# A fused adaLN block on one Trainium2 core: shift and scale moved to the features, projections with half-row pairs, gate rows in four column tiles, and a new list of steps

## The chip, the cores and the metric

The kernel runs on one core of a Trainium2 chip. A core has a matrix engine (TensorE, PE in the profile, with its weight loads shown apart as PEld), a vector engine (VectorE, DVE), a scalar engine (ScalarE, ACT), GpSimd (POOL) and SyncE (SP), which here issues nearly all DMA transfers. The metric is the device time of one execution in microseconds; 416.89 is the median before.

## What is computed

Everything is bfloat16, for one batch of 2048 tokens with 576 features and 32 heads of 18:

```python
mod = (silu(c) @ w_mod)            # six rows of 576: sa, ca, ga, sb, cb, gb
h = layernorm(x) * (1 + ca) + sa
q, k, v = split(h @ wqkv)          # 32 heads of 18
phi(t) = concat(softmax(t @ w_phi), softmax(-(t @ w_phi)))
o = phi(q) @ (phi(k).T @ v) / (phi(q) @ sum(phi(k)))
x = x + ga * (o @ wo)
h = layernorm(x) * (1 + cb) + sb
x = x + gb * (relu(h @ w1) @ w2)   # 576 -> 4608 -> 576
```

The attention is linear: the keys of all tokens are summed into one small matrix per head before any query can be finished. So all 16 tiles of 128 tokens go through the norm, the key and value projections and the key softmax first. Then the queries and the FFN run in blocks of two tiles.

## The kernel before

**Two parts.** The first is a list of short steps, written out by hand as a string (L900) and run through a table of lambdas (L857): DMA loads, folding of weights, norms, projections, key softmax, key-value sums, and attention and FFN of the first block. The second, `block(n)` (L928), runs the other seven blocks in loops. The scheduler is off for SyncE, TensorE, VectorE and ScalarE (`manual_schedule`), so each of these engines executes its instructions in the order of the list. An instruction that waits holds up all that is behind it on its engine, and nothing on another unless it waits for that one. The order between engines comes from semaphores alone.

**Folded weights.** The query and key weights are multiplied by `w_phi` on the chip: the raw key weights are transposed on TensorE (`fold_T`, L333; the query weights arrive transposed by DMA, `load_turned`, L156), multiplied with a block-diagonal `wbd` (`fold`, L343), and copied out (`fold_out`, L350). The factor 1 + ca is then multiplied into the rows of the folded weights and of the value weights (`fold_scale`, L355, steps SC1, SCv, SC0), and the shift sa is turned into one row per weight (`fold_bias`, L362, steps B1, Bv, B0; copied by BE1, BEv, BE0) that sits in row 64 of the fifth chunk. The normalised tile has a one in column 576 to meet it. The 576 features are thus four chunks of 128 rows and a fifth of 64 rows, padded with the shift row and zeros.

**The norm.** Statistics per tile on VectorE (LS, L217), the root on ScalarE (RS, L223), the normalisation per pair of tiles on VectorE (LX, L227). Tiles 0 to 3 are transposed on TensorE (PT, L248) and copied out by ScalarE and VectorE (PTA, PTB); tiles 4 to 15 by DMA (LT, L242). The features hT1 have three buffers of four tiles.

**Projections.** `project` (L546) makes K, V or Q of one tile: two halves of the columns by five chunks, ten matmuls into one of three PSUM buffers (`mmp`, L74; L425 in the profile). ScalarE copies each out (KE, VE, QE). K and Q have column parts of 270 and 306, V of 288 and 288.

**Key softmax.** Per block of four tiles: minimum and maximum trees (MN, MX), differences (LO, HI) on VectorE, exponentials on ScalarE (EX, L484), sums on TensorE (SU, L491), the last addition (SA), reciprocals on ScalarE (RC), scaling on VectorE (SC). Steps with q do the same for the queries of a block. KVa to KVc sum keys times values (L603), KVE copies them out. NU, NUE, OT, OTE, WO, WOE carry the first block on; S2, R2, X2, PN, PNE are its second norm; G and FW are its FFN (L785, L793).

**Gates.** The gate ga is multiplied into the columns of `wo` (`wo_scale`, L390), gb into the FFN's output. Both rows are needed on all partitions, so a matmul with the SiLU vector repeated 128 times (`crep`) makes each (`mod_row`, L377, steps RA and RB; L382 in the profile).

In the FFN, the chunk of 64 rows is already handled in pairs (`f1_pairs`, L780; `wo_pair`, L686): two matmuls of 64 rows each, one on the upper and one on the lower half of the array's rows, into different PSUM banks.

## Time and profile before

| | us |
|---|---|
| median of three runs | 416.89 (416.82 to 417.81) |
| the profiled execution | 416.77 |
| its span, first to last instruction | 414.8 |
| TensorE busy | 406.0 |
| VectorE busy | 237.0 |
| ScalarE busy | 173.8 |
| first K projection starts | 16.26 |
| key-value sums start | 84.68 |
| first FFN matmul starts | 103.61 |

Rows of groups give line, engine, operation, the tiles written and read, shapes and count, then the time in which the group was busy, the mean duration of one in ns, and the idle time of the engine just before them with what ended it. In a timeline the first two columns are start and length. The length of a merged row reaches to the end of its last instruction, and matmuls overlap, so the cost of a matmul in a stream is read from one start to the next. A row of a stretch gives its bounds and length, then busy time and count of TensorE, of its weight loads, of VectorE, ScalarE and GpSimd, then the granted TensorE clock (1.00 is full), the DMA share and GB/s.

### The profile page before, as it was taken

The numbers are of one execution on the slowest core, as the hardware profiler recorded it, in microseconds if no ns is written. First come the engines' busy times: TensorE is split into PE (matmuls) and PEld (weight loads), VectorE is DVE, ScalarE is ACT, GpSimd is POOL, SyncE is SP. The second block draws the span as 40 slices with busy tenths as digits, with TensorE's granted clock in tenths as the row PEclk, the third lists the DMA queues.
The fourth block names the chain that finished last, engine by engine and source line by source line (L and its number), as shares of the span: only waits on it lengthen the run. The fifth ranks groups of instructions, "written<-read, shape, count | busy, mean of one in ns | idle before, by whom it ended". The sixth has DMA issues, their size and how long they took to land.

```text
span 414.8 us, 9278 instructions
## 1 busy us (share of the span) xinstructions
PE 406.0 (98%) x3993; PEld 332.4 (80%) x3993; DVE 237.0 (57%) x617; ACT 173.8 (42%) x280; POOL 12.0 (3%) x39
## 2 busy tenths in 40 slices
PE   6899999999999999999999999999999999999997
PEld 4777877787887888788878887888888788878876
DVE  7989999988855554637345552746192533230011
ACT  4787889954861064006302630452055014302400
POOL 8100000000000000000000000000000000000000
PEclk9999999999999999999999999999999999999999
DMA  8959665079561420613051014203210501210000
GB/s 254 255 142 276 127 176 120 2 188 363 204 163 27 101 63 2 83 48 33 12 107 32 16 33 85 46 2 67 65 34 2 115 17 32 14 33 16 2 0 30
DMA packets 70513, 35.12 MB, mean 85 GB/s; under 512 B 55305, under 2 KB 68106, under 8 KB 70474
## 3 DMA queue, kind: packets, MB, share of 16 engines
q1 hardware_dynamic: 69872, 34.52, 35.3%
q8 instruction: 31, 0.51, 0.5%
q10 hardware_dynamic: 602, 0.02, 0.1%
q14 instruction: 8, 0.07, 0.0%
...
## 4 chain that ended last, share of the span: by engine, by line
PE 94%; DVE 3%; DMA 1%; ACT 1%; issue 0%; SPq 0%; ACTq 0%
PE ps_y L836 34%; PE ps_h L793 31%; PE ps_q L425 5%; PE ps_v L425 4%; PE ps_h L785 4%; PE ps_k L425 4%; PE ps_sum L491 3%; PE ps_wo L701 3%; PE ps_wo L425 2%; PE ps_kv L603 1%; PE ps_num L644 1%; DMA wk_raw<-in_A_wqkv_dram 1%; PE ps_wT L337 1%; PE ps_row L382 1%; DVE xn L229 1%
## 5 line engine op out<-in xcount | busy, mean ns | idle before, releaser
L798 ACT ACTIVATE H<-ps_h 128x1024 bf16<-128x1024 f32 x72 | 73.6, 1022 | 170.8 <-PE ps_h L785 120.9
L836 PE MATMUL ps_y<-w_sb,H 128*128 128x288 bf16 (+2 forms) x1188 | 143.0, 282 | 0.0
L836 PEld LDWEIGHTS <-H 128*128 128x128 bf16 x1188 | 113.7, 98 | 27.3
L793 PE MATMUL ps_h<-hT,w1a 128*128 128x256 bf16 x640 | 74.9, 273 | 0.4 <-DVE hT L396 0.4
L793 PEld LDWEIGHTS <-w1a 128*128 128x128 bf16 x640 | 61.2, 98 | 10.1 <-issue 2.8
L844 DVE TENSOR_TENSOR outt<-ps_y,row_gb 128x288 bf16<-128x288 f32 (+2 forms) x33 | 14.8, 448 | 86.8 <-PE ps_y L836 86.8
L793 PE MATMUL ps_h<-hT,w1b 128*128 128x256 bf16 x512 | 59.0, 273 | 0.0
L425 PEld LDWEIGHTS <-hT 128*128 128x128 bf16 x480 | 46.1, 97 | 12.7 <-issue 0.9
L793 PEld LDWEIGHTS <-w1b 128*128 128x128 bf16 x512 | 49.8, 98 | 6.6 <-issue 0.6
L706 DVE TENSOR_TENSOR x_sb<-x_sb,ps_wo 128x288 bf16<-128x288 bf16 x28 | 12.7, 454 | 33.5 <-PE ps_wo L701 24.8
L220 DVE BATCH_NORM_STATS2 bst<-x_sb 128x6 f32<-128x288 bf16 x64 | 25.6, 442 | 0.2
L229 DVE TENSOR_SCALAR xn<-x_sb,mv,rstd 128x576 bf16<-128x576 bf16 x32 | 12.2, 424 | 21.7 <-ACT rstd L225 21.6
L425 PE MATMUL ps_v<-wv_sb,hT 128*128 128x288 bf16 x160 | 21.6, 286 | 0.3 <-ACT wv_sb L358 0.3
L425 PE MATMUL ps_k<-wfold,hT 128*128 128x270 bf16 (+1 forms) x160 | 21.4, 285 | 0.4 <-ACT wfold L86 0.4
L425 PE MATMUL ps_q<-wfold,hT 128*128 128x270 bf16 (+1 forms) x160 | 21.4, 285 | 0.0
L502 DVE TENSOR_REDUCE ln_s<-room 128x66 f32<-128x1188 bf16 x14 | 19.1, 1368 | 3.3 <-ACT room L484 3.3
L785 PE MATMUL ps_h<-hT,w1c 64*128 64x256 bf16 x288 | 19.9, 271 | 0.0
L484 ACT ACTIVATE room<-room 128x1188 bf16<-128x1188 bf16 x16 | 18.9, 1196 | 0.5
L484 ACT ACTIVATE phik<-phik 128x2376 bf16<-128x2376 bf16 x8 | 17.5, 2184 | 0.4 <-DVE phik L457 0.4
L785 PEld LDWEIGHTS <-w1c 64*128 64x128 bf16 x288 | 12.1, 94 | 5.1 <-issue 3.8
L444 DVE TENSOR_TENSOR tree<-tree 128x264 bf16<-128x264 bf16 (+2 forms) x48 | 14.6, 304 | 1.7
L396 DVE TENSOR_SCALAR hT<-hT,mod 128x256 bf16<-128x256 bf16 x35 | 9.7, 343 | 6.4 <-DMA hT<-xn 6.4
...
## 6 DMA issues: line engine op xcount, KB each, us to landing
...
```

Of the source, the lines that this page charges most:

```text
L220: V.bn_stats(out=st[:, half, :], in_=x_sb[:, t0 + j, half * 288:(half + 1) * 288])
L229: V.tensor_scalar(out=xn[:, j, 0:D], in0=x_sb[:, t0 + j, :], scalar1=mv[:, j, 0:1], scalar2=rs[:, j:j + 1], op0=ALU.subtract, op1=ALU.mult)
L425: T_.matmul(ps[:, 0:cn], lhsT=lhs[:, ci, :], rhs=w[:, ci, cs:cs + cn], start=(ci == 0), stop=(ci == KC - 1))
L444: V.tensor_tensor(out=a[:, :, 0:w], in0=a[:, :, 0:w], in1=a[:, :, w:2 * w], op=op)
L484: A_.activation(out=E[:, j:j + k], in_=E[:, j:j + k], func=ACT.Exp)
L502: V.tensor_reduce(out=t["l", b][:, k * 22:(k + 1) * 22].rearrange("p (g s) h -> p g s h", s=2), op=ALU.add, axis=mybir.AxisListType.X, in_ ...
L706: V.tensor_tensor(out=xs[:, cs:cs + cn], in0=xs[:, cs:cs + cn], in1=p[:, 0:cn], op=ALU.add)
L785: T_.matmul(f1[q][:, e, hh * w:hh * w + w], lhsT=w1["c"][r, 2 * q + hh, :], rhs=hT[r, 4, :], start=(first and hh == 0), stop=(not first an ...
L793: T_.matmul(f1[q][:, e, hh * w:hh * w + w], lhsT=w1_at(2 * q + hh, e, ci), rhs=hT[:, ci, :], start=(first and hh == 0 and ci == 0), stop=( ...
L798: A_.activation(out=p2t["H1"].rearrange("p (e j) n -> p e j n", e=2)[:, :, 2 * q:2 * q + 2], in_=f1[q][:].rearrange("p e (h n) -> p e h n" ...
L836: T_.matmul(ps[:, 0, 0:cn], lhsT=p2t["H1"][:, k, j * P:(j + 1) * P], rhs=p2t["w2"][:, k, c], start=(k == 0), stop=(k == NJ - 1))
L844: V.tensor_tensor(out=o[:, c], in0=ps[:, 0, 0:cn], in1=rows["gb"][:, c], op=ALU.mult)
```

## The change

The features are cut differently: chunks begin at 0, 128, 256, 320 and 448, and the third holds 64 features (256 to 319) twice, on the lower and the upper 64 partitions. The normalised tile is written with these 64 columns doubled (`spread`), per tile and on VectorE or ScalarE, so its transpose has them on both halves. Folding writes the middle chunk twice in two column tiles, and the loads follow the new cut.

Shift and scale are applied to the transposed features: for tiles 0 to 3 while they leave PSUM (PX, per pair of tiles and chunk), for the others in place (MH, per block and chunk). The steps SC1, SCv, SC0, B and BE are gone, and `wfold` and `wv_sb` are filled directly. A fourth buffer for the features of the last block is taken from the ET buffers.

`project` takes two (tile, kind) numbers: 0 to 15 are K, 16 to 31 V, 32 to 47 Q, step J.a.b. It runs the eight whole matmuls of the first, the pair of half-row matmuls of the first, the pair of the second, and its eight whole ones. The pair uses the two row halves for the two column halves.

The two gate rows become one step (RW): four column tiles of 32, each a half of ga or gb, then one copy (RWE), a store of four rows to DRAM and two broadcast loads (RD.2, RD.0, RD.1). The gate scaling of `wo` is two operations instead of five. The list is a new one throughout; the loops after it are as they were.

```diff
+CS = [0, 128, 256, 320, 448]
+CK = [P, P, 64, P, P]
+HC = 2
...
+    def load_values(i):
+        if i < 2:
+            rows = A_wqkv[i * 320:i * 320 + 256, 2 * D:].rearrange("(k p) n -> p k n", p=P)
+            nc.sync.dma_start(wv_sb[:, 3 * i:3 * i + 2, :], rows)
+        else:
+            for h in range(2):
+                cols = slice(2 * D + h * 288, 2 * D + h * 288 + 288)
+                nc.sync.dma_start(wv_sb[h * 64:h * 64 + 64, HC, h * 288:h * 288 + 288], A_wqkv[256:320, cols])
 
...
+        def spread(j, eng):
+
+            row = x_sb[:, t0 + j, :]
+            src = bass.AP(row.tensor, row.offset, [list(row.ap[0]), [256, 2], [1, 320]])
+            dst = xn[:, j, :].rearrange("p (a n) -> p a n", a=2)
+            if eng is A_:
+                nm = work.tile([P, 1], FP32, name="nm", tag="nm", bufs=4)
+                V.scalar_tensor_tensor(out=nm[:], in0=mv[:, j, 0:1], scalar=-1.0, in1=rs[:, j:j + 1], op0=ALU.mult, op1=ALU.mult)
+                A_.activation(out=dst, in_=src, func=ACT.Identity, scale=rs[:, j:j + 1], bias=nm[:])
+            else:
+                V.tensor_scalar(out=dst, in0=src, scalar1=mv[:, j, 0:1], scalar2=rs[:, j:j + 1], op0=ALU.subtract, op1=ALU.mult)
+
...
     def hT_of(b):
+        if b == 3 and b not in hT1:
+            t = work.tile([P, NG, U, P], BF16, name="hT3", tag="ET", bufs=2)
+            hT1[b] = t[:].rearrange("p g u c -> p (g u c)")[:, 0:KC * TPB * P].rearrange("p (k n) -> p k n", k=KC)
         if b not in hT1:
...
+    def ln1_out(u, ci, eng):
         c0 = u % 2 * U * P
-        for c1, c2 in parts:
-            copy(eng, hT_of(u // 2)[:, c1:c2, c0:c0 + U * P],
-                 psT[u][:, c1 * U * P:c2 * U * P].rearrange("p (k n) -> p k n", n=U * P))
-
+        modulate(eng, hT_of(u // 2)[:, ci, c0:c0 + U * P], psT[u][:, ci * U * P:(ci + 1) * U * P], mod[1], ci)
+
+    def ln1_mod(b, ci, eng):
+        modulate(eng, hT1[b][:, ci, :], hT1[b][:, ci, :], mod[1], ci)
 
...
-            for ck in range(KC):
-                o = (ck * 2 + r) * D + ci * P
-                T_.matmul(mod_ps[1][:, r * KC + ci:r * KC + ci + 1], lhsT=wma_[:, o:o + P], rhs=siluc[:, ck, :],
-                          start=(ck == 0), stop=(ck == KC - 1))
+            for p in range(0, P, CK[ci]):
+                for ck in range(KC):
+                    o = (ck * 2 + r) * D + CS[ci]
+                    T_.matmul(mod_ps[1][p:p + CK[ci], r * KC + ci:r * KC + ci + 1], lhsT=wma_[:, o:o + CK[ci]], rhs=siluc[:, ck, :],
+                              start=(ck == 0), stop=(ck == KC - 1))
+
+    mod[1] = const.tile([P, 2, KC], FP32, name="mod1")
...
         for g in range(NGR):
             nf = G6 if g < 5 else 2 * DH
-            T_.matmul(ps[0:KK[ci], g // 4, (g % 4) * G6:(g % 4) * G6 + nf], lhsT=wT[which][0:G6, g, ci * P:ci * P + KK[ci]],
-                      rhs=wbd[0:G6, g, 0:nf], start=True, stop=True)
+            for p in range(0, P, CK[ci]):
+                T_.matmul(ps[p:p + CK[ci], g // 4, (g % 4) * G6:(g % 4) * G6 + nf], lhsT=wT[which][0:G6, g, CS[ci]:CS[ci] + CK[ci]],
+                          rhs=wbd[0:G6, g, 0:nf], start=True, stop=True)
 
...
+    def gate_rows():
+        ps = rows["ps"] = mm_tile("ps_row")
+        for ck in range(KC):
+            for k in range(4):
+                o = k // 2 * 3 * D + k % 2 * 288
+                T_.matmul(ps[k * 32:k * 32 + 32, 0, 0:288], lhsT=crep[:, ck, :], rhs=wmb[:, ck, o:o + 288],
                           start=(ck == 0), stop=(ck == KC - 1))
 
-    def mod_row_out(name):
-        r = const.tile([P, D], BF16, name=f"row_{name}")
-        copy(A_, r[:].rearrange("p (a n) -> p a n", a=2), rows[name][:, :, 0:288])
-        rows[name] = r
-
-    def wo_scale(ci):
-        V.tensor_tensor(out=wo_sb[:, ci, :], in0=wo_sb[:, ci, :], in1=rows["ga"][:], op=ALU.mult)
+    def gate_rows_out(eng):
+        rows["four"] = wqp.tile([P, 288], BF16, name="row_four")
+        copy(eng, rows["four"][:], rows["ps"][:, 0, 0:288])
+
+    def gate_row(i):
+        if i == 2:
+            nc.sync.dma_start(four_d[:], rows["four"][0:P:32, :])
+            return
+        name = ("ga", "gb")[i]
+        r = rows[name] = const.tile([P, D], BF16, name=f"row_{name}")
+        nc.sync.dma_start(r[:].rearrange("p (a n) -> p a n", a=2), four_d[2 * i:2 * i + 2].unsqueeze(0).to_broadcast([P, 2, 288]))
+
+    def wo_scale(i):
+        c = slice(0, 2) if i == 0 else slice(2, KC)
+        V.tensor_tensor(out=wo_sb[:, c, :], in0=wo_sb[:, c, :], op=ALU.mult,
+                        in1=rows["ga"][:].unsqueeze(1).to_broadcast([P, c.stop - c.start, D]))
 
...
-    def project(name, t, w):
-        b, j = t // TPB, t % TPB
-        ps = pss[name, t] = mm_tile("ps_" + name)
-        proj((ps[:, 0], ps[:, 1]), hT1[b][:, :, j * P:(j + 1) * P], w, HALVES if name == "v" else PARTS)
+    WSRC = (("k", wfold[1], PARTS), ("v", wv_sb, HALVES), ("q", wfold[0], PARTS))
+
+    def project(*at):
+
+        def opened(k):
+            kind, w, splits = WSRC[k // NT]
+            t = k % NT
+            ps = pss[kind, t] = mm_tile("ps_" + kind)
+            return ps, hT1[t // TPB][:, :, t % TPB * P:t % TPB * P + P], w, splits
+
+        def whole(ps, lhs, w, splits, first):
+            for i, (cs, cn) in enumerate(splits):
+                for ci in (0, 1, 3, 4):
+                    T_.matmul(ps[:, i, 0:cn], lhsT=lhs[:, ci, :], rhs=w[:, ci, cs:cs + cn],
+                              start=(first and ci == 0), stop=(not first and ci == 4))
+
+        def pair(ps, lhs, w, splits, first):
+            for i, (cs, cn) in enumerate(splits):
+                r = slice(i * 64, i * 64 + 64)
+                T_.matmul(ps[:, i, 0:cn], lhsT=lhs[r, HC, :], rhs=w[r, HC, cs:cs + cn], start=first, stop=not first)
+
+        open_ = []
+        for k in at[:-1]:
+            open_.append(opened(k))
+            whole(*open_[-1], True)
+        last = opened(at[-1])
+        for p in open_:
+            pair(*p, False)
+        pair(*last, True)
+        whole(*last, False)
...
+    LP.1 LP.0 LK.1 LS.0 LS.2 WT.4 LK.0 WT.1 LH WBD WTE.4.1 WTE.1.1 WT.3 WTE.3.1 LS.1 RS.0 LP4.2 LS.3 F1.4 SIL
+    LS.4 RS.1 FB1.4.1 Z.11 Z.10 WT.0 F1.3 FA1.4.1 LX.1 LS.6 LS.7 LK.2 LA.0 LA.1 LV.0 Z.4 F1.1 FA1.3.1 FB1.3.1
+    MC1.0 LX.3 WTE.0.1 LX.0 WT.2 FA1.1.1 FB1.1.1 MSH WTE.2.1 F1.0 FA1.0 RS.3 MC1.1 FB1.0.1 MSC PT.0 PX.0.0.1
+    PX.0.3.1 Z.0 LQ.5 LX.2 PT.1 PX.0.4 LQ.0 LQ.1 F1.2 PX.1.1.1 OPEN CR PX.1.0 PX.0.2 LP4.4 PX.0.1.1 LV.1 PM.2
+    PM.1 PX.1.2 PM.0 PX.1.4 FB1.2 PX.1.3.1 FA1.2.1 J.0.1 KE.0 LX.7.1 LV.2 KE.1 J.16.17 LS.5 LX.6.1 VE.0 RS.2
+    LQ.3 LQ.2 LS.8 LS.9 LQ.4 F0.2 LS.10 LS.11 F0.0 RS.4 VE.1 FA0.2.1 LX.5 FB0.2 F0.3 LX.8.1 FA0.0 FB0.0 FB0.3.1
+    FA0.3.1 LX.9.1 RS.5 LP4.6 LX.4 LS.15 LS.14 LT.7 LT.6 LS.13 J.2.3 LT.5 LT.4 KE.2 LM.1 KE.3 J.18.19 VE.2
+    MH.1.0 MH.1.1 MH.1.3.1 VE.3 F0.1 FB0.1.1 FA0.1.1 MH.1.4 MH.1.2 J.6.7 KE.6 MN.0 KE.7 LX.10 LT.8 LT.9 LT.10
+    LX.11.1 F0.4 FB0.4.1 FA0.4.1 LS.12 J.4.5 KE.4 RS.7 J.34.35 MX.0 LO.0 MC2.3 LX.15 KE.5 RS.6 QE.2 LT.11 MH.2.0
+    MH.2.1 MH.2.4.1 QE.3 LX.14.1 J.32.33 MH.2.2.1 LX.12.1 MC2.0 MC2.2 LM.2 LO.1 MC2.4 MH.2.3 LX.13 LT.13 QE.1
+    MN.1 QE.0 HI.0 J.10.11 KE.10 J.8.9 EX.0 KE.8 KE.11 LO.2 KE.9 MX.1 LO.3 HI.3 SU.0 EX.3 LT.15 J.26.27 LT.14
+    LT.12 MH.3.1 qMX.0 PM.3 HI.1 SA.0 MH.3.0 MC2.1 LM.0 RW VE.10 MH.3.4 MH.3.2 MH.3.3.1 VE.11 J.12.13 MCE2 HI.2
+    SU.3 RC.0 MN.2 W1 RWE.1 LO.5 MX.2 KE.12 EX.2 KE.13 J.14.15 SA.3 SC.0 KE.14 RD.2 KE.15 qHI.0 J.20.21 VE.4
+    RC.3 LO.4 HI.5 HI.4 qMN.0 qLO.0 VE.5 EX.1 SU.2 J.22.23 VE.6 EX.5 J.30.31 VE.14 VE.7 SA.2 SU.5 qEX.0 VE.15
+    EX.4 qEX.1 MN.3 MX.3 J.24.25 LO.7 VE.8 HI.7 SC.3 RC.2 SU.1 LW.1.1 J.28.29 SA.1 VE.12 SA.5 RC.5 LO.6 HI.6
+    RC.1 VE.9 SU.4 LW.0.0 SC.5 qSU.0 qSA.0 SA.4 LW.2.0 EX.6 SC.2 EX.7 RD.0 VE.13 WOL qMN.1 RC.4 RD.1 qRC.0
+    J.40.41 QE.8 QE.9 SU.6 SU.7 SC.1 J.44.45 SA.6 qSC.0 SA.7 SC.4 KVa QE.12 RC.6 QE.13 SC.6 RC.7 SC.7 KVb KVc
+    KVE.0.1 WS.0 J.42.43 QE.10 KVE.1 qT.0 WS.1 NU.0 NUE.0 qLO.1 NU.1 QE.11 LW.1.0 J.38.39 QE.6 OT.0 NUE.1 OT.1
+    qMX.1 OTE.0 WO.0 OTE.1 WO.1 WOE.0 QE.7 J.36.37 QE.4 WOE.1 S2.1 S2.0 R2 QE.5 J.46.47 QE.14 X2 LW.2.1 P2
+    W2.1.1 LW.0.1 LW.3.0 PN PNE qMX.2 qHI.1 QE.15 G.0 W2.2.0 FW.2 RL.0 qEX.2 RL.2 W2.1.0 qEX.3 qMN.2 FW.1 RL.1
+    qHI.2 G.1 qSD.2 W2.0.0 qSD.3 qRC.1 RL.3 FW.4 LW.3.1 W2.0.1 FW.5 qSC.1 qT.1 qLO.2 RL.4 qEX.5 RL.5 G.2 RL.6
+    FW.8 NV.0 NVE.0 FW.7 Y.0.0.0 OU.0 NV.1 RL.7 NVE.1 OU.1 W2.2.1 Y.0.0.1 WP.0 Y.1.0.0 Y.1.0.1 WPE.0 qEX.4 RL.8
+    WP.1 Y.0.0.2 qSD.4 S3.0 Y.1.1.0 qSD.5 Y.1.1.1 WPE.1 S3.1 R3 qRC.2 YE.0.0 Y.1.0.2 Y.0.1.0 qSC.2 X3 XT MD.2
+    MD.3 Y.1.1.2 Y.0.1.1 qT.2 YE.1.0 MD.1 MD.4 Y.0.1.2 MD.0 YE.1.1 YE.0.1
```

In the new list a trailing .1 of a copying or modulating step means ScalarE and its absence VectorE.

More of the change, by code (lines that the diff above doesn't have):

```diff
@@ L371, in fold_bias_out @@
-    def fold_bias_out(which, dst, half, eng):
-        p = 64 - half * 64
-        copy(eng, dst[64:65, 4, half * 288:(half + 1) * 288], pool_tiles["B", which][p:p + 1, half, 0:288])
-    rows = {}
-    def mod_row(name, i):
-        ps = rows[name] = mm_tile("ps_row")
-        for half in range(2):
-            for ck in range(KC):
-                o = i * D + half * 288
-                T_.matmul(ps[:, half, 0:288], lhsT=crep[:, ck, :], rhs=wmb[:, ck, o:o + 288],
-                          start=(ck == 0), stop=(ck == KC - 1))
```

104 lines of the change are left out of this document (26 added, 78 removed).

## The prediction, as put on record

> **What bounds the kernel now.** I read the busy shares first, then the stretches between landmarks, then the groups, then the TensorE timeline around the few places where it already works in parts of its array.
>
> ```profile
> PE 406.0 (98%) x3993; PEld 332.4 (80%) x3993; DVE 237.0 (57%) x617; ACT 173.8 (42%) x280; POOL 12.0 (3%) x39
> PE 94%; DVE 3%; DMA 1%; ACT 1%; issue 0%; SPq 0%; ACTq 0%
> ```
>
> TensorE is busy for 98% and carries 94% of the chain that ended last, at a granted clock of 1.0 throughout. So TensorE time taken out counts, as long as nothing else is late. The stretches (first column the time, then TensorE, its weight loads, VectorE, ScalarE) show where that is tight:
>
> ```profile
> 16.26:28.56 12.30, 11.82 (x111) 9.44 (x111) 11.12 (x33) 10.24 (x29) 0.62 (x3) 1.00 0.72 175
> 28.56:54.03 25.47, 25.47 (x254) 20.06 (x252) 24.15 (x65) 18.78 (x43) 1.03 (x3) 1.00 0.74 177
> 54.03:84.68 30.65, 30.65 (x249) 23.53 (x247) 29.75 (x55) 29.14 (x49) 0.00 (x0) 1.00 0.40 103
> 84.68:103.61 18.93, 18.57 (x313) 15.71 (x309) 15.33 (x40) 9.12 (x25) 0.00 (x0) 1.00 0.98 295
> ```
>
> The first K starts at 16.26, the key-value sums at 84.68, the first FFN matmul at 103.61; all after that is untouched by the change but for the order of a few steps. From 28.56 to 84.68 TensorE never idles, and VectorE (53.9 of 56.1 us) and ScalarE (47.9) have little room. What the change does to the start of the FFN, it does to the time.
>
> **What is exchanged.** Gone: 15 weight scalings, 30 one-row matmuls and six one-row copies for the shift, six copies of transposed tiles, one of two gate copies and five gate scalings. Added: 10 modulations of 256 columns, 15 of 512, two gate scalings over 1152 and 1728 columns (by L455, 0.77 for 1188, some 0.7 and 1.05), seven normalisations moved to ScalarE, each with a one-column product on VectorE (0.1). SyncE issues two more loads for the value weights and three for the gate rows, 0.5 to 0.6 each.
>
> **The projections.** One projection is 10 matmuls; L425 rows in the timeline stand 1.225 apart. A pair is priced from the FFN, where the same kind of pair runs:
>
> ```profile
> 189.27 1.15 PE L793 MATMUL ps_h<-hT,w1a 128*128 128x256 bf16 x9
> 190.34 0.83 PE L785 MATMUL ps_h<-hT,w1c 64*128 64x256 bf16 x12
> 191.01 0.29 PE L691 MATMUL ps_wo<-wo_sb,oT 64*128 64x288 bf16 x2
> 191.23 1.15 PE L701 MATMUL ps_wo<-wo_sb,oT 128*128 128x288 bf16 x8
> 192.22 0.60 PE L793 MATMUL ps_h<-hT,w1a 128*128 128x256 bf16 x4
> ```
>
> Twelve half-row matmuls start within 0.67 us: six pairs at 0.11, so two do run at once. But nine whole ones need 190.34 − 189.27 = 1.07 where 9 x 0.109 (16 in 1.75 in the chain) is 0.98: 0.09 for entering. The pair at 191.01 has its successor 0.22 later where a 288-wide matmul takes 0.1225: 0.10 for leaving. Two changes of the array's division cost 0.19 to 0.20 per visit. One J step makes one visit for two projections: 16 whole matmuls 1.96, two pairs 0.26 (K and Q are 270 and 306 wide, the wider sets it, 0.13) or 0.245 (V), visit 0.195: 2.415 or 2.40 against 2.45. Sixteen K and Q steps save 0.035 each, eight V steps 0.05: 0.95 us together.
> [...]
>
> **Gate rows.** Two steps of 10 matmuls (27.01 to 28.23, and again at 52.81) are 2.45 us. The new step has 20 in four column tiles: five rounds. The removed shift rows show two column tiles at once, 10 matmuls from 33.55 to 34.26:
>
> ```profile
> 33.55 0.78 PE L368 MATMUL ps_bias<-room 128*1 128x288 bf16 x10
> 34.26 1.40 PE L425 MATMUL ps_v<-wv_sb,hT 128*128 128x288 bf16 x10
> ```
>
> The same line's weight loads (ns min/median/max):
>
> ```profile
> L368 PEld LDWEIGHTS <-room x30: 79/83/84, 13.4 to 33.9; 128*1 128x1 bf16 x30
> ```
>
> Five rounds of 0.1225 plus a visit: 0.81, saving 1.65. No row shows four tiles. If only two run at once it is 1.42; if the 20 weight loads of 0.083 went one by one, 1.66 + 0.2. I take four, since the two are exactly two. Bounds of the saving: 0.6 to 1.65.
> [...] The 83 ns here are no longer than the 98 ns of whole loads, and they hid.
>
> **Shift rows gone.** B1 and Bv lie before the first K in dependency time; B0 is in the dense stretch and goes from 33.46 to 34.26: 0.80 saved. The middle chunk's fold in two column tiles adds one visit, 0.2, while query weights are folded. Dense work: −0.95 − 1.65 − 0.80 + 0.2 = −3.2.
>
> **The start.** A 576 KB load of x now stands ahead of the modulation weights (issued 5.46, some 5.4 to landing, so about 11.4 before). The DMA moves about 340 GB/s there, so 0.59 MB is 1.75 us: 13.1. Their matmuls (25 in 0.63 before, now 30 and a visit, 0.95) end at 14.1, the add at 14.5 where it was 13.06. VectorE gets there at the same time: from the landing of tile 0 (4.9) seven statistics at 0.93, feature maps and SiLU 1.25, four small steps and three normalisations at 0.36 make 9.6. Then four modulations of 128x256 run on ScalarE at 0.45 to 0.5 (0.56 alone at L395), so the features of tiles 0 and 1 are there at 16.7: 0.45 later than 16.26. The last half-chunk fold's copy (17.5) is needed only by the pair, at 17.8. Next, the value weights: the old ones landed at 13.4; one x load (1.75), three transposed loads (about 0.8 each) and another x load (1.75) go ahead of the last two pieces: 19.5, while J.0.1 ends at 19.1. Stall 0.4, about the 0.48 idle of the old stretch. Query folds wait for the last transposed load, 22.0, when J.16.17 ends. LX.4 ends on VectorE near 24.1, its transpose lands 3 us later, five modulations follow: tiles 4 to 7 are ready at 28.6, when TensorE has done eight projections and four query folds. The old list had seven and the folds at 28.56.
>
> **VectorE and ScalarE in the dense part.** Gone from VectorE after 28.6: five statistics (4.65), three normalisations (1.1), three weight scalings (1.0), four gate scalings (1.7, moved to the tail, where it idles 3.6), a fold copy (0.6). Added: seven modulations of 128x512 (0.35, between 0.26 for 256 in L396 and 0.36 for 576 in L229, start to start), one softmax root (1.5), small ones 0.2. Net −4.9: 49.0 in a stretch of 51.7. ScalarE: +2.2 for three normalisations of 640 (0.74), +2.0 for modulations, −1.5 scalings, −0.8 shift copies, −0.9 gate copies, −1.9 evictions that come later: 47.0. Walking the list step by step, both arrive in time, some by 0.1 to 0.2. LM.0, issued near 43, lands near 47.5, before RW at 48.5. RD.2 waits on SyncE for RW's copy (50.4); only FFN weights queue behind it, and the gate is read 30 us later.
>
> **The tail.** Four J steps (9.65) instead of seven projections (8.58) follow the key-value sums; the second quotient comes 0.5 after TensorE asks for it, since VectorE does WS and a softmax root between. That step of 1.06 is inside the −3.2; the 0.5 is extra. qT.0 needs the buffer beside block 3's features, free; its landing (about 84) is before the first numerator (88).
>
> Sum: −3.2 + 0.45 − 0.1 + 0.5 = −2.35. The profiled execution took 416.77, span 414.8 and 2.0 around it, 0.12 under the median of 416.89. 416.77 − 2.35 = 414.4; in the median's terms 414.5. I add 0.1 for lateness of the closest copies: **414.6**. With the bounds of the gate rows (+1.05), of the start (−0.5 to +0.8) and no lateness the case runs from 413.6 to 415.8.
>
> **Rivals.**
> A, slower: a J step holds two of three PSUM buffers. A buffer must be emptied within 2.2 us (the end of one pair to the next use), where single projections gave 2.45. An exponential (66.38 to the next start at 68.46, 2.08) ahead of a copy (0.58, and 0.1 of signalling) is 2.76: 0.5 late, for each of eight exponentials. +4.0: 418.6. From five such places on the gain is gone, from seven it is slower by 0.3%. For it: ScalarE had 29.14 of 30.65 busy. Against: the same order of sizes left TensorE no idle before, and sums of 1.19 stand between most J steps. 0.20.
> B: the normalisation reads two overlapping 320s. If VectorE does this at the rate of the crep copy (640 in 0.81) rather than of L229 (576 in 0.42), nine cost 3.5 more; 1.5 are spare: 416.6. For: no row has such a source. Against: L455 has patterns of four dimensions and takes 0.65 ns an element, half of crep's 1.27. 0.12.
> C: the transposed loads ahead of the value weights take their issue time of 1.39 rather than 0.8, and J.16.17 waits 1.7 more: 416.3. 0.12.
> [...]
> E: forecast, 0.54.
>
> **Chances.** No change that is under 0.3% (1.25 us) can be told here. Faster: E but for 0.02 at its upper end, D, and 0.06 of B and C, whose early ends reach below 415.6: 0.60. Same: that 0.02 and 0.16 of B and C: 0.18. Slower: A and 0.02 of C with a longer queue: 0.22. The range, 413.4 to 418.0, leaves out D and three quarters of A, 0.17; E alone is 413.6 to 415.8.
>
> **What would show it.** K at 16.7, values from 19.6; J steps 2.40 to 2.42 apart; one ps_row group of 0.6; the key-value sums at 80.5 and the FFN at 101.2. Wrong if TensorE shows idle on ScalarE copies between 50 and 80 (A), xn takes 0.7 or more (B), or ps_v waits on a DMA past 20 (C).

## The result, and the profile after

The changed kernel is slower: 419.62 us (median of 18, 418.62 to 421.83) against 417.50 (18, 416.78 to 418.65), a ratio of 1.0060 with a 95% interval of 1.0048 to 1.0073. The forecast was 414.6, with a range from 413.4 to 418.0. Single executions of one kernel lie up to 4.9 us apart (e13, 416.27 to 421.14), and every trace with a span of 417.5 or more has TensorE at half rate in parts of the stretch from 10 to 25 us (eight equal matmuls in up to 2.10 there instead of 1.14), so times are compared here by their medians, and a milestone from one trace can hold 1 to 2 us of that.

The profiled execution took 419.59, span 417.5. Busy times and the chain that ended last:

```profile
PE 404.1 (97%) x3987; PEld 322.1 (77%) x3987; DVE 232.8 (56%) x610; ACT 178.3 (43%) x286; POOL 7.4 (2%) x27
PE 91%; DMA 1%; ACT 0%; DVE 0%; issue 0%; SPq 0%
```

TensorE has 1.9 us less to do (404.1, before 406.0), and the span is 2.7 longer. The stretches after (bounds and length, then TensorE, its weight loads, VectorE, ScalarE, GpSimd, granted clock, DMA) say where: up to the first K, to J.6.7 (the K projections of tiles 6 and 7), to the key-value sums, to the first FFN matmul.

```profile
10.00:19.31 9.31, 5.63 (x124) 4.95 (x123) 7.42 (x27) 6.06 (x17) 1.15 (x8) 1.00 1.17 262
19.31:32.73 13.42, 12.89 (x110) 8.18 (x110) 10.66 (x38) 11.39 (x27) 0.00 (x0) 0.87 0.73 138
32.73:84.70 51.97, 51.97 (x481) 35.58 (x479) 49.64 (x110) 49.52 (x92) 0.87 (x2) 1.00 0.46 122
84.70:105.51 20.81, 20.08 (x325) 15.41 (x322) 15.31 (x34) 9.33 (x28) 0.00 (x0) 1.00 1.01 299
```

| | forecast | after | before |
|---|---|---|---|
| first K | 16.7 | 19.31 | 16.26 |
| J.6.7 | 28.6 | 32.73 | |
| J.6.7 to key-value sums | 51.9 | 51.97 | |
| key-value sums | 80.5 | 84.70 | 84.68 |
| to the first FFN matmul | 20.7 | 20.81 | 18.93 |
| first FFN matmul | 101.2 | 105.51 | 103.61 |
| from there to the end of the span | 311.2 | 312.0 | 311.2 |

So 4.1 of the 5.1 us between forecast and span are lost before J.6.7, 0.8 behind the start of the FFN, and 0.2 in all that lies between.

Rows of TensorE's timeline from 14 to 23 us, and of the waits of all engines from 10 to 20, show the start:

```profile
14.51 1.03 PE L328 MATMUL ps_mod<-siluc,wma 128*128 128x1 bf16 x30 [1.51 <-DVE mod L337]
19.31 1.14 PE L572 MATMUL ps_k<-wfold,hT 128*128 128x270 bf16 x8 [2.04 <-ACT hT L408]
20.38 0.69 PE L578 MATMUL ps_k<-wfold,hT 64*128 64x270 bf16 x4
21.01 2.10 PE L572 MATMUL ps_k<-wfold,hT 128*128 128x270 bf16 x8
```

```profile
PE ps_k L572 <- ACT hT L408: 2.0, 1, 2.0
PE ps_mod L328 <- DVE mod L337: 1.5, 1, 1.5
DVE hT L409 <- ACT hT L408: 1.1, 1, 1.1
ACT hT L408 <- DVE hT L409: 1.1, 1, 1.1
```

The second modulation matmuls wait until VectorE has read the shift from the first, which lies in the same PSUM tile and behind other work on VectorE. Then the ten modulations of tiles 0 to 3 alternate between ScalarE and VectorE, and each engine waits 1.1 for the other, though they write different chunks: they read one PSUM tile. The order was kept for the whole tile: VectorE waited with chunk 4, where ScalarE had only chunks 0 and 3 of that tile ahead of it. What asks for this order, the chip or the program alone, is not shown. And TensorE, idle for 2 us, then runs slower: eight whole matmuls take 1.14, the next eight 2.10.

The dense stretch is what was forecast, although ScalarE has 49.5 us to do in it and not 47.0. A K step and a V step, and the gate rows with their neighbours:

```profile
32.73 1.14 PE L572 MATMUL ps_k<-wfold,hT 128*128 128x270 bf16 x8
35.44 1.14 PE L572 MATMUL ps_k<-wfold,hT 128*128 128x270 bf16 x8
52.54 0.80 PE L386 MATMUL ps_row<-wmb,crep 128*32 128x288 bf16 x20
53.27 1.16 PE L572 MATMUL ps_k<-wfold,hT 128*128 128x270 bf16 x8
68.97 1.14 PE L572 MATMUL ps_v<-wv_sb,hT 128*128 128x288 bf16 x8
72.57 1.14 PE L572 MATMUL ps_v<-wv_sb,hT 128*128 128x288 bf16 x8
```

35.44 − 32.73 = 2.71 holds a J step and a fold of 0.27: 2.44. 72.57 − 68.97 = 3.60 holds a J step and a group of sums of 1.19: 2.41. The gate rows take 53.27 − 52.54 = 0.73, where one of the two old steps took 1.23.

Behind the start of the FFN:

```profile
132.94 0.90 PE L875 MATMUL ps_y<-w_sb,H 128*128 128x288 bf16 x6
134.28 11.19 PE L875 MATMUL ps_y<-w_sb,H 128*128 128x288 bf16 x90 [0.43 <-DMA w_sb<-in_B_w_dram]
```

The last of the six `w_sb` loads (W2.2.1) now stands behind OU.1 in the list. OU.1's transposes wait on SyncE for the quotients of the second block of queries, so the load goes out at 129.16 instead of 117.03, and TensorE reaches the weights first.

### The profile page after: what moved, and what is told of

The parts are those of the page before. It is cut to its first block, busy times and chain, and to the rows that moved or that the text cites. A ratio compares the mean times of both kernels' runs of the same rounds, so it can differ in the third digit from the quotient of the medians.

```text
span 417.5 us, 9262 instructions
## 1 busy us (share of the span) xinstructions
PE 404.1 (97%) x3987; PEld 322.1 (77%) x3987; DVE 232.8 (56%) x610; ACT 178.3 (43%) x286; POOL 7.4 (2%) x27
## 4 chain that ended last, share of the span: by engine, by line
PE 91%; DMA 1%; ACT 0%; DVE 0%; issue 0%; SPq 0%
PE ps_y L875 33%; PE ps_h L832 31%; PE ps_h L824 4%; PE ps_q L572 4%; PE ps_k L572 4%; PE ps_v L572 3%; PE ps_wo L740 3%; PE ps_sum L504 3%; PE ps_wo L438 2%; DMA w_sb<-in_B_w_dram 1%; PE ps_kv L642 1%; PE ps_num L683 1%; PE ps_q L578 1%; PE ps_k L578 1%; PE ps_v L578 1%; PE ps_wo L730 0%
## 5 line engine op out<-in xcount | busy, mean ns | idle before, releaser
L572 PEld LDWEIGHTS <-hT 128*128 128x128 bf16 x384 | 35.5, 99 | 17.5 <-issue 8.5
L572 PE MATMUL ps_k<-wfold,hT 128*128 128x270 bf16 (+1 forms) x128 | 19.2, 296 | 2.4 <-ACT hT L408 2.0
L572 PE MATMUL ps_v<-wv_sb,hT 128*128 128x288 bf16 x128 | 18.6, 291 | 0.0
L572 PE MATMUL ps_q<-wfold,hT 128*128 128x270 bf16 (+1 forms) x128 | 18.2, 286 | 0.2 <-ACT room L92 0.2
L237 DVE TENSOR_SCALAR xn<-x_sb,mv,rstd 128x576 bf16<-128x576 bf16 x16 | 6.1, 427 | 20.1 <-ACT rstd L233 20.1
L409 DVE TENSOR_SCALAR hT<-hT,mod 128x256 bf16<-128x256 bf16 (+1 forms) x46 | 13.7, 359 | 6.3 <-DMA hT<-xn 6.2
## 6 DMA issues: line engine op xcount, KB each, us to landing
w1b<-in_B_w_dram SPq DMA_DIRECT2D x2, 1024.0 KB, 12.2
```

The costliest lines, as they stand in the source:

```text
L409: return V.tensor_scalar(out=dst, in0=src, scalar1=mod[:, 1, ci:ci + 1], scalar2=mod[:, 0, ci:ci + 1], op0=ALU.mult, op1=ALU.add)
L572: T_.matmul(ps[:, i, 0:cn], lhsT=lhs[:, ci, :], rhs=w[:, ci, cs:cs + cn], start=(first and ci == 0), stop=(not first and ci == 4))
```

## Experiments

Theory S: the loss is the late start (PSUM hand-overs, then the slow TensorE) and the late load, and the dense stretch is as forecast. Rival D: the dense stretch, with two of three PSUM buffers held by a J step, costs, and the start only moves its waits.

The edits show pieces of the list of steps, with "..." for what is left out. MC1.0 and MC1.1 are the modulation matmuls for shift and scale, MSH and MSC read them out of PSUM. F1 and F0 fold key and query weights, FA and FB copy the two column parts of a fold out. LP and LP4 load x, LQ the transposed query weights, LV the value weights. ZN.n is n matmuls on zeros, 512 columns each.

### The two hand-overs at the start

e1 moves the shift's read next to the scale's; e2 gives each of the two transposed tiles to one engine; e3 does both.

```diff
 # e1
-FB1.1.1 MSH WTE.2.1
+FB1.1.1 WTE.2.1
-FB1.0.1 MSC PT.0
+FB1.0.1 MSH MSC PT.0
 # e2
-PT.0 PX.0.0.1 PX.0.3.1 ... PX.0.4 ... F1.2 PX.1.1.1 OPEN CR PX.1.0 PX.0.2 ... PX.0.1.1 ... PX.1.2 ... PX.1.4 ... PX.1.3.1 FA1.2.1 J.0.1
+PT.0 ... PX.0.0 PX.0.1 PX.0.3 PX.0.4 PX.0.2 ... F1.2 OPEN CR FA1.2.1 PX.1.0.1 PX.1.1.1 ... PX.1.2.1 PM.0 PX.1.3.1 PX.1.4.1 FB1.2 J.0.1
```

> The changed kernel, with one step moved in the list: the reading of the shift columns (MSH) stands right ahead of the reading of the scale (MSC), behind both modulation matmul groups. In the changed kernel the second group started at 14.51, 0.05 after MSH ended on VectorE, though the weights had landed and TensorE had been idle for 1.5 us: both groups write one PSUM tile. Theory S (the start is late, and TensorE's clock fell over it; the dense stretch is as forecast): the second group starts near 13.1, the scale is there 0.5 earlier (15.1, then VectorE's own queue sets it), the first K starts near 18.8 instead of 19.31, and the time falls by 0.4 to 0.6 us. Rival D (the dense stretch is what costs: steps that hold two of three PSUM buffers, with ScalarE behind): the key-value sums stay at 84.7 and the time within 0.3 us.

> The changed kernel, with the ten modulations out of PSUM shared out otherwise: those of tiles 0 and 1 all on VectorE, those of tiles 2 and 3 all on ScalarE, and the copy of the last folded chunk ahead of the latter on ScalarE. In the changed kernel VectorE waited 1.11 us for ScalarE and ScalarE 1.06 us for VectorE within the same PSUM tile. Theory S: these waits go, five modulations of 0.32 follow the scale directly, and the first K starts near 17.8 instead of 19.31; TensorE idles less than 1 us before it, so its granted clock falls less; time lower by 1.5 to 2.8 us. Rival D: first K earlier, but the key-value sums still near 84.7 and the time within 0.5 us.

> The changed kernel with both edits: the shift is read behind the second modulation group, and each pair of tiles is modulated by one engine. Theory S: first K near 17.3, the key-value sums at 81.5 to 82.5, time lower by 2.0 to 3.6 us than the changed kernel's, so 416 to 417.5. Rival D: no more than 0.7 us lower.

Measured (the kernel before: 417.22): e1 418.86, ratio 1.0039 (1.0022 to 1.0055); e2 419.54, 1.0051 (1.0034 to 1.0069); e3 418.13, 1.0013 (1.0000 to 1.0025). Against the changed kernel's 1.0060 (1.0048 to 1.0073) only e3 is clearly told apart. e2 missed its 1.5 to 2.8 us, and e3, 1.5 lower than the changed kernel, lies between its two expectations. In e1 the modulation matmuls no longer wait. In e2 and e3 neither engine waits for the other at the PSUM tiles, although both still write one tile of features, so it was the PSUM tile that put one behind the other. In e3, stretches and one wait:

```profile
17.92:31.50 13.58, 11.53 (x114) 7.64 (x111) 10.85 (x39) 12.88 (x31) 1.15 (x8) 1.00 0.88 150
31.50:83.46 51.96, 51.96 (x482) 35.56 (x479) 49.62 (x110) 49.47 (x92) 0.87 (x2) 1.00 0.45 123
```

```profile
PE ps_fold L372 <- ACT v L92: 1.4, 2, 1.0
```

The first K comes 1.4 earlier than in the changed kernel, J.6.7 1.2, the sums 1.2. With both hand-overs removed the gain reaches the end, and the stretch of 52.0 stays as it is, against D. How much of the 1.2 is theirs alone is not shown: TensorE has a slow spell in both traces, here before the first K (ten transposes in 1.23 instead of 0.72), in the changed kernel behind it. And TensorE now waits at the query folds, since their PSUM buffers are emptied by ScalarE, which has all of PX.1 and two normalisations ahead of them. One late step was in front of another.

### How fast TensorE runs

e4 adds matmuls on zeros ahead of the second modulation matmuls and of the first K:

```diff
-F1.0 FA1.0 RS.3 MC1.1
+F1.0 FA1.0 RS.3 ZN.6 MC1.1
-PX.1.3.1 FA1.2.1 J.0.1
+PX.1.3.1 FA1.2.1 ZN.8 J.0.1
```

> The changed kernel with matmuls on zeros in TensorE's two idle stretches ahead of the first K: six of 512 columns ahead of the second modulation group and eight ahead of the first J step. Nothing is made earlier. Theory S: the granted clock in 20 to 30 us stays at 1.00 instead of 0.83, the first J step takes 2.4 us instead of 3.6 and the second 2.4 instead of 2.9; first K at 19.3 to 19.5; time lower by 1.0 to 1.7 us. Rival D: the clock stays up, but the steps after it wait for ScalarE and VectorE, and the time moves by less than 0.4 us.

419.01, ratio 1.0035 (1.0021 to 1.0048). The row of the first K, and that of e1, whose profiled execution ran slowly from the start:

```profile
21.78 1.14 PE L572 MATMUL ps_k<-wfold,hT 128*128 128x270 bf16 x8 [0.20 <-ACT hT L408]
```

```profile
20.26 2.08 PE L572 MATMUL ps_k<-wfold,hT 128*128 128x270 bf16 x8 [1.40 <-ACT hT L408]
```

With the wait filled, both first J steps run at full rate, and from first K to J.6.7 it is 12.2 (21.78 to 33.98) instead of 13.42: 1.2 us are the slow spell's. The median gains 0.6, less than the 1.0 to 1.7 expected: the fills themselves were slow in the traced execution (six in 2.5, where the eight ahead of the first K took 1.9) and put off what they stood in front of.

e10 puts six fills into the idle time ahead of the first transposes (2.4 to 5.1) of the changed kernel, e9 into that of e8 below.

```diff
-LS.0 LS.2 WT.4
+LS.0 LS.2 ZN.6 WT.4
```

> The changed kernel with the same six matmuls on zeros and nothing else. Theory S: its waits for the PSUM tiles stay (first K at 19 to 19.5), but the slow stretch at 10 to 18 goes, the one behind the long wait for the first K may stay: 418.6 to 419.3, a spread under 1.5 where the changed kernel has 418.6 to 421.8. Rival P: as the changed kernel, 419.6, spread 3.

> e8 with six more matmuls on zeros ahead of the first transpose of key weights, in time that TensorE spends waiting for them (3 to 5.7). Theory S: in e6 the times fell into two groups, 415.9 to 417.5 and 419.4 to 419.8, as eight whole matmuls take 1.14 or 2.08 in the first J step; busy early, TensorE should be at its full rate by the modulation matmuls (30 in 1.03, not 1.20) in every execution: all times between 415.2 and 416.6, median 0.3 to 0.8 below e8. Rival P (the rate at the start does not depend on how busy TensorE was): the same two groups, median as e8.

e10: 420.86, ratio 1.0069 (1.0044 to 1.0094); e9: 418.90, 1.0037 (1.0017 to 1.0057), where e8 has 417.80. Both expectations missed: more work early did not keep TensorE fast. The times spread as wide (416.01 to 420.70 in e9); e9 is 1.1 longer than e8, and e10 is not told apart from the changed kernel. The rate changes by a factor near two (eight equal matmuls in 1.14 or 2.08). The waits of TensorE ahead of slow spells are 1.3 to 2.0 in six traces (the changed kernel, e2, e5, e8, e10, e16), but 0.2 in e3 and 0.5 in e13, and behind 1.9 in e9 there is no spell. The fills, 2.74 long, did not bring full rate sooner: in e10 a fold at 10.37 still took 0.69, in the changed kernel without the fills one at 10.19 took 0.43. Why, stays open.

### The late load

```diff
-qSC.1 qT.1 qLO.2
+qSC.1 qT.1 W2.2.1 qLO.2
-NVE.1 OU.1 W2.2.1 Y.0.0.1
+NVE.1 OU.1 Y.0.0.1
```

> Only the last of the six w_sb loads moves, from behind OU.1 to right behind qT.1 in the list (on SyncE from about 129.2 to about 119.3). Theory S (start late, and this load late): the ps_y wait of 0.43 on the DMA at 134.28 and the break at 132.94 go; first FFN matmul stays at 105.5, block 1 begins 0.7 us earlier relative to it (39.1 instead of 39.8), time 0.6 to 0.8 below the changed kernel: 418.8 to 419.0 where that is at 419.6. Rival N (the load only looks late; something else, VectorE or a buffer, holds the same place): less than 0.2 us.

419.14, ratio 1.0046 (1.0029 to 1.0064). The row of TensorE that was broken:

```profile
133.78 11.92 PE L875 MATMUL ps_y<-w_sb,H 128*128 128x288 bf16 x96
145.54 1.69 PE L832 MATMUL ps_h<-hT,w1a 128*128 128x256 bf16 x14
```

The wait is gone; from the first FFN matmul (106.35) to block 1 it is 39.19 instead of 39.79. 0.6 us, at the lower end.

### The pairs

```diff
-                r = slice(i * 64, i * 64 + 64)
-                T_.matmul(ps[:, i, 0:cn], lhsT=lhs[r, HC, :], rhs=w[r, HC, cs:cs + cn], start=first, stop=not first)
+                T_.matmul(ps[:, i, 0:cn], lhsT=lhs[:, HC, :], rhs=w[:, HC, cs:cs + cn], start=first, stop=not first)
...
+    V.memset(wv_sb[:, HC, :], 0.0)
```

> The changed kernel without the half-row pairs: the middle chunk is multiplied as one matmul of 128 rows per column half (the value weights' unused quarters are zero, so V is unchanged; for K and Q the 64 features count twice). Theory S: a J step takes 20 x 0.1225 = 2.45 instead of 2.44 (K, Q) and 2.41 (V); from J.6.7 to the key-value sums 52.0 becomes 52.4, the time 0.4 to 0.6 above the changed kernel. By the price in the forecast (0.95 for all 24 steps) it would be 0.95 above it. Rival D (changes of the array's division stall the engine more than the pairs save): the time falls.

421.15, ratio 1.0094 (1.0072 to 1.0117). From J.6.7 (34.10) to the sums (86.46) it is 52.36, 0.39 more than with pairs. This stretch has 16 of the 24 steps (ten K and Q, six V), for which the forecast's prices give 0.65, so S is right by its size. The median is 1.5 above the changed kernel's, more than S allows. Against e16 below, whose traced execution also starts slowly and reaches J.6.7 at 34.19, this one is only 0.34 longer (421.25, 420.91). So the rest lies before J.6.7, in the rate of the start and the added memset, which are not separated here.

### A start without these waits

From e6 on the list is rewritten up to J.6.7, always with e5's load. The core of each:

```diff
 # e6: transposes first, shift beside scale, PX on VectorE, copies and normalisations reordered
-FB1.1.1 MSH WTE.2.1 F1.0 FA1.0 RS.3 MC1.1 FB1.0.1 MSC PT.0
+FB1.1.1 WTE.2.1 F1.0 FA1.0 RS.3 PT.0 MC1.1 FB1.0.1 MSH MSC
+LX.2 PX.0.0 PX.0.1 PX.0.3 PX.0.4 PX.0.2 ... F1.2 FA1.2.1 FB1.2.1 LX.7.1 LX.6.1 PX.1.0 PX.1.1 PX.1.2 PX.1.3 PX.1.4
+KE.0 KE.1 J.16.17 LS.5 RS.2 VE.0 ... LP4.6 LT.7 LT.6 F0.2 LX.5 LX.4 LT.5 LT.4 ... LS.15 LS.14 LS.13 J.2.3
 # e8, against e6
-LS.4 ... LX.1 LX.0 LS.6 LS.7 ... LX.3 ... MSH MSC LX.2 PX.0.0
+LX.1 LX.0 ... LS.4 ... LX.3 LX.2 LS.6 LS.7 ... MSH MSC PX.0.0
-F0.0 VE.1 FA0.2 FB0.2 F0.3 RS.4 FB0.3.1 FA0.3.1 FA0.0 FB0.0 ... J.2.3
+F0.0 VE.1 FA0.2 FB0.2 RS.4 J.2.3 KE.2 LX.8.1 KE.3 FA0.0 FB0.0 F0.3
 # e11, against e8
-MC1.1 MSH MSC ... PT.1 LQ.0 LQ.1 F1.2 FA1.2.1 FB1.2.1
+MC1.1 F1.2 FA1.2.1 FB1.2.1 MSH MSC ... PT.1 LQ.0 LQ.1
-LS.15 LS.14 LS.13 LM.1 J.18.19 ... MH.1.2 J.6.7
+LS.15 LM.1 J.18.19 ... MH.1.2 LS.14 LS.13 J.6.7
```

> The changed kernel with the start of the list rewritten: transposes of tiles 0 and 1 ahead of the second modulation matmuls, the shift read beside the scale read, all ten modulations of tiles 0 to 3 on VectorE, the last half-chunk fold copied by ScalarE, ScalarE's first two normalisations ahead of the K copies, normalisations of tiles 4 and 5 and their transposed loads ahead of the statistics of tiles 10 to 15, and the w_sb load of e5. Theory S: first K at 17.0 to 17.5, J.6.7 at 29.3 to 30 (32.7 in the changed kernel, 31.5 in e3), key-value sums at 81.3 to 82.2, first FFN matmul at 102.1 to 103, the rest as in e5: span 413.4 to 414.5, 415.4 to 416.5, that is 1 us or more below the kernel before. Rival D (the dense stretch itself costs, and the start only moves its waits): J.6.7 at 31 or later or the stretch from J.6.7 to the key-value sums longer than 52.2, time not under 417.2.

> e6 with the start rewritten once more: normalisations of tiles 0 to 3 ahead of the statistics of tiles 4, 6 and 7 on VectorE, the last 128-row key fold copied by ScalarE, the third query fold behind the first J step of tiles 2 and 3, the second key fold's evictions in that order on ScalarE. Theory S (what is left is start): first K at 16.9 to 17.2 (17.80 in e6), the wait of 0.8 before the second K step under 0.2, J.6.7 at 28.6 to 29.4 (29.89 in e6), key-value sums at 81.0 to 82.0, span 413.3 to 414.2; 415.3 to 416.2 where TensorE starts at its full rate, and some 3 more where it does not. Rival D: J.6.7 comes earlier and the key-value sums do not.

> e8 with the last 128-row key fold ahead of the transposes of tiles 2 and 3, and the statistics of tiles 13 and 14 on VectorE behind the modulations of tiles 4 to 7 instead of ahead of them: in e8 VectorE reached these 1.3 us after ScalarE had begun the first, and TensorE waited 1.89 for them at 29.9. Theory S: first K at 16.3 to 16.6, J.6.7 at 28.3 to 28.9, no wait over 0.7 between, eight whole matmuls 1.14 in all J steps from there on; key-value sums at 80.3 to 80.9, first FFN matmul at 101.1 to 101.8: the milestones of the forecast (80.5 and 101.2); span 412.4 to 413.2, 414.3 to 415.2, a spread under 2. Rival D: the statistics come due later in the dense stretch, TensorE waits there for VectorE between 40 and 80, key-value sums not before 81.5.

| | first K | J.6.7 | key-value sums | median | ratio to before |
|---|---|---|---|---|---|
| changed kernel | 19.31 | 32.73 | 84.70 | 419.62 | 1.0060 (1.0048 to 1.0073) |
| e6 | 17.80 | 29.89 | 82.47 | 416.59 | 1.0000 (0.9977 to 1.0024) |
| e8 | 16.63 | 29.91 | 83.79 | 417.80 | 1.0002 (0.9986 to 1.0017) |
| e9 (e8, filled) | 16.32 | 29.74 | 82.01 | 418.90 | 1.0037 (1.0017 to 1.0057) |
| e11 | 15.60 | 29.04 | 83.57 | 418.10 | 1.0019 (1.0006 to 1.0031) |

e6 recovers the loss: its median is 3.0 lower than the changed kernel's, its lowest and highest times are 2.8 and 2.0 lower, so it is not only that fewer executions run slowly. 2.2 of the 2.8 at J.6.7 reach the sums. The stretch between them is longer than the 52.2 named for D, but TensorE idles only 0.24 in it, and the time is under 417.2:

```profile
29.89:82.47 52.58, 52.34 (x481) 35.71 (x479) 50.07 (x112) 49.51 (x92) 1.01 (x2) 1.00 0.47 119
```

The first K, the sums and the FFN came 0.3 later than expected. Of its twelve times eight lie between 415.87 and 417.47 and four between 419.37 and 419.79, so it is not told apart from the kernel before. e8 and e11 bring the first K another 1.2 and 2.2 earlier and gain nothing by it; their expectations missed. The waits of TensorE in e8 and in e11 from 10 to 60 us:

```profile
PE ps_k L572 <- DVE hT L409: 1.9, 1, 1.9
PE ps_k L572 <- ACT wfold L92: 0.8, 1, 0.8
```

```profile
PE ps_q L572 <- ACT wfold L92: 1.4, 1, 1.4
PE ps_k L572 <- DVE hT L409: 1.0, 1, 1.0
PE ps_v L572 <- DMA wv_sb<-in_A_wqkv_dram: 0.8, 1, 0.8
PE ps_mod L346 <- DMA wmb<-in_w_mod_dram: 0.5, 1, 0.5
```

And of VectorE from 20 to 33 us and SyncE's queue in e11:

```profile
DVE hT L409 <- DMA hT<-xn: 0.9, 1, 0.9
20.38 6.38 SPq L267 DMA_TRANSPOSE hT<-xn  x4
```

Each wait that goes uncovers the next: the modulations of tiles 4 to 7 behind statistics on VectorE (e8), then the same modulations behind their transposed loads, whose issue takes SyncE from 20.4 to 26.8 (e11), the value weights, and the copy of the last query fold, which ScalarE has behind a normalisation whose one-column product VectorE makes after two statistics and a tree (e11). In the traced execution of e8 the wait of 1.9 was again followed by a slow spell (granted clock 0.83 from 30 to 40). In that of e9, the same list with fills far ahead, the same wait was not. From J.6.7 to the sums e8 takes 53.88 and e9 52.27, so the spell cost 1.6. The second eight matmuls behind the wait, first e8, then e9:

```profile
31.79 2.10 PE L572 MATMUL ps_k<-wfold,hT 128*128 128x270 bf16 x8
31.49 1.16 PE L572 MATMUL ps_k<-wfold,hT 128*128 128x270 bf16 x8
```

e12 aims at three of e11's waits, e13 goes back to e8 and moves other steps.

```diff
 # e12, against e11
-OPEN LP4.4 LV.1 PM.2 PM.1 PM.0 J.0.1 LV.2 KE.0 KE.1 J.16.17 LS.5 RS.2 VE.0
+OPEN LV.1 LV.2 LP4.4 PM.2 PM.1 PM.0 J.0.1 LS.5 KE.0 RS.2 KE.1 J.16.17 LX.5 LX.4 VE.0
-LQ.4 LP4.6 LT.7 LT.6 F0.2
+LQ.4 LT.7 LT.6 LP4.6 F0.2
-J.6.7 KE.6 MN.0 KE.7 LX.10 LT.8 LT.9 LT.10 LX.11.1 F0.4 FB0.4.1 FA0.4.1 LS.12
+J.6.7 KE.6 KE.7 F0.4 FB0.4.1 FA0.4.1 LX.10 LT.8 LT.9 LT.10 LX.11.1 MN.0 LS.14 LS.13 LS.12
 # e13, against e8
-FA0.2 FB0.2 RS.4 J.2.3 KE.2 LX.8.1 KE.3 FA0.0 FB0.0 F0.3
+FA0.2 FB0.2 RS.4 FA0.0.1 FB0.0.1 J.2.3 KE.2 LX.8.1 KE.3 F0.3
+J.6.7 KE.6 KE.7 F0.4 FB0.4.1 FA0.4.1 LX.10 ... LX.11.1 MN.0 LS.13 LS.12
```

> e11 with three waits of its trace taken out of the list: the last value weights ahead of the third load of x on SyncE (V waited 0.76 for them), normalisations and transposed loads of tiles 4 and 5 ahead of the statistics of tiles 8 and 9 and of the last load of x, the last query fold copied by ScalarE ahead of its normalisation of tile 11 and the key softmax's first tree behind the normalisation of tile 10 (J.34.35 waited 1.39). Theory S (waits of the list): first K at 15.5 to 16, V without a wait over 0.3, J.6.7 at 28 to 28.7, J.34.35 without a wait over 0.4, from J.6.7 to the key-value sums 52.0 to 52.6, those at 80.3 to 81.3, first FFN matmul at 101.1 to 102.1; 414.3 to 415.5. Rival V (VectorE, over 95% busy from 30 to 80, is the second bound: it cannot get through its statistics, trees and differences sooner, whatever the list): TensorE waits elsewhere between 30 and 50, over 53 from J.6.7 to the key-value sums, those not before 82, 416 or more.

> e8 with one query fold copied by ScalarE instead of VectorE (0.9 less there), the statistics of tile 13 behind the modulations of tiles 4 to 7, the last query fold copied ahead of ScalarE's normalisation of tile 11, the first tree behind the normalisation of tile 10. If it was the order (theory S): first K at 16.6, J.6.7 at 28.3 to 28.9 (29.9 in e8), no wait of TensorE over 0.5 from there, key-value sums at 80.6 to 81.3, 414.6 to 415.6. If VectorE is the second bound (rival V): J.6.7 as early, but TensorE waits between 30 and 80, key-value sums at 81.6 to 82.6, VectorE idle about 2.3 from 28 us on, 415.7 to 416.7.

e12: 417.99, ratio 1.0015 (0.9999 to 1.0031); e13: 416.78, 1.0008 (0.9982 to 1.0034), nine times between 416.27 and 417.01 and three above 420. Both missed their expectations. In e12 two of the three waits are gone (for the value weights, and of J.34.35), the one for the features of tiles 4 to 7 stays at 1.0, and others stand beside it:

```profile
PE ps_fold L372 <- DMA room<-in_A_wqkv_dram: 1.2, 1, 1.2
PE ps_k L572 <- DVE hT L409: 1.0, 1, 1.0
PE ps_mod L346 <- DMA wmb<-in_w_mod_dram: 0.6, 1, 0.6
PE ps_row L386 <- ACT v L92: 0.6, 1, 0.6
```

The value weights, moved ahead, made the third load of x and with it the transposed query weights later. The DMA share is 1.15 from 10 us to the first K and 0.95 from there to J.6.7: a load put first puts another last.

### Is VectorE a second bound?

Rival V: with 50 of 52 us busy from J.6.7 to the sums, VectorE would let no earlier start through. e14 is e13 with half the columns in the statistics of tiles 8 to 15; e15 is e11, and e16 the changed kernel, with two steps of each key softmax tree left out, so the roots are taken over a part of the features.

```diff
 # e14
+        sw = 144 if xn is not None and t0 >= 8 else 288
-                V.bn_stats(out=st[:, half, :], in_=x_sb[:, t0 + j, half * 288:(half + 1) * 288])
+                V.bn_stats(out=st[:, half, :], in_=x_sb[:, t0 + j, half * 288:half * 288 + sw])
 # e15, e16
-            for w in (2 * G2, G2):
+            for w in ((2 * G2, G2) if n < 4 else ()):
```

> e13 with the statistics of tiles 8 to 15 taken over half the columns (this leaves out half of the features in their mean and variance): 2 x 0.15 to 0.2 less on VectorE per tile, 2.4 to 3.2 in all, most of it before 35 us; nothing changes for TensorE. Theory S: the key-value sums come at most 0.3 earlier than in e13, since TensorE is the bound from J.6.7 on. Rival V: they come 0.8 us or more earlier, and TensorE's waits between 28 and 80 get shorter by that.

> e11 with two of the five steps left out of each of the key softmax's eight minimum and maximum trees (so the root is taken over a part of the features): some 0.8 less on VectorE each, 6 in all between J.6.7 and the key-value sums; TensorE and ScalarE do the same as in e11. Rival V (VectorE second bound): TensorE's idle of 2.5 between J.6.7 and the sums goes to under 1, the stretch from 54.5 to 52.9 or less, the sums to 82.0 or earlier, time 1.5 to 2 below e11. Rival L (single late steps and loads): only the wait of 1.39 at J.34.35 gets shorter, by 0.8 at most; the time at most 0.8 below e11.

> The changed kernel with the same two steps left out of the eight trees, nothing else. TensorE never idles there between J.6.7 and the key-value sums, so both views expect that stretch at 52.0 and the time at the changed kernel's 419.6 within 0.4, with VectorE idle for 8 instead of 2.3 in it. If the time falls by 1 or more, VectorE holds up TensorE in a way that the waits do not show.

e14: 416.26, ratio 0.9981 (0.9961 to 1.0001), 0.5 below e13 and between the two expectations; its profiled execution was one of those that start slowly, where the sums stand at 85.81 and in e13 at 85.83, so its trace doesn't decide. e15: 417.46, 0.6 below e11. Its waits of TensorE from 10 to 84 us:

```profile
PE ps_k L572 <- DVE hT L409: 0.9, 1, 0.9
PE ps_v L572 <- DMA wv_sb<-in_A_wqkv_dram: 0.7, 1, 0.7
PE ps_q L572 <- ACT wfold L92: 0.6, 1, 0.6
PE ps_mod L346 <- DMA wmb<-in_w_mod_dram: 0.5, 1, 0.5
```

5.7 us less work on VectorE (46.33, from 51.99) shorten the stretch by 0.83 (53.70, from 54.53), which is the one wait behind the first tree, 1.4 to 0.6. That is rival L: single late steps and loads, and V falls. In e16 the stretch is 51.96 as in the changed kernel, as both views had it. Its median, 420.62, is 1.0 above the changed kernel's, where 0.4 was allowed, but the ratio, 1.0072 (1.0053 to 1.0091), does not tell them apart.

## Why the prediction was wrong, and where it was right

**Wrong: the step headed "The start".** It had the features of tiles 0 and 1 at 16.7 and eight projections with four folds done at 28.6; they came at 19.31 and 32.73. Three things were missed in it.
- The hand-overs at PSUM tiles: 1.5 at the modulation, 1.1 twice between ScalarE and VectorE. I added up each engine's own instructions as if the two read one PSUM tile side by side, where each waited 1.1 for the other. The profile before had the sign of it: ScalarE's copies of transposed tiles waited twice, 2.0 in all, for VectorE's copies of the same tiles (`ACT hT L86 <- DVE hT L88: 2.0, 2, 1.5`). e3 shows it: without them the first K comes 1.4 earlier and the median is 1.5 lower. The transposes of tiles 0 and 1 also stand behind the late modulation matmuls on TensorE, and ScalarE waited 0.9 for them.
- TensorE's rate: J.0.1 and J.16.17 took 3.59 and 2.94 (19.31 to 22.90 to 25.84) where two steps at full rate take 4.8: 1.7 lost behind a wait of 2 us. e4 shows 1.2 of it. The first J step runs at half rate in part also in the traces of e1, e2, e5, e7, e10 and e16, so this is no single accident of one execution. The forecast had every matmul at full rate.
- What comes next: with K in time, TensorE meets copies of folds, features of tiles 4 to 7 and loads that are each some tenths to 1.9 late. LX.4, put at 24.1, ran at 28.3, since VectorE waited 1.6 for a root and 0.9 for a fold's copy, both on ScalarE. The forecast of 28.6 for those features was near what the lists reach at best (29.04 in e11), but it had no place for the others.

**Wrong: a queue not looked at.** The step that let "only FFN weights queue behind" SyncE's wait in the dense part checked one place on that queue and not W2.2.1 behind OU.1: 0.8 by the trace, 0.6 by e5.

**A slip in the sum.** From its own terms the case runs from 414.0 (414.5 − 0.5, no lateness) to 416.5 (414.6 + 1.05 + 0.8), not from 413.6 to 415.8. The measured time lies outside both.

**Right in mechanism and near in size.** The J steps: 2.44 for K and Q (forecast 2.415), 2.41 for V (2.40); so the pairs save less than 0.95 over all 24 steps, some 0.5, and e7 shows 0.39 for the 16 between J.6.7 and the sums. The gate rows: 0.73 (0.81), four column tiles at once; its 20 weight loads, 92 to 97 ns each, took 0.49 together, beside the matmuls. The dense stretch: 51.97 (51.9). The tail: 20.81 (20.7).

**The rivals.** A, ScalarE and PSUM buffers at 418.6, had the sign and nearly the time, but not the place: TensorE does not idle between 32.73 and 84.70. Its mechanism appears only in the start, at the query folds (0.2 in the changed kernel, 1.4 in e3). B is out: normalisations with the doubled columns take 0.4 on VectorE. C is out here, since no value projection waits for a load; in e11 it does, for 0.8. The 0.8 that the forecast has for a transposed load was the author's estimate: in the changed kernel SyncE took 5.70 and 4.31 to issue two groups of three. The D of its chances, that the changes of the array's division cost nothing, is out too: 16 whole matmuls and two pairs would then take 1.96 + 0.26 = 2.22, and a K or Q step took 2.44.

**Open:** what decides in which executions TensorE starts at half rate, and whether a list exists that reaches 80.5 at the sums. The best traced here is 82.01 (e9, 416.01 in that execution), and no version was measured faster than the kernel before beyond its interval.
